# Kernel rows of a long convolution: two channels per matmul, group 2's rows and skip term earlier, one butterfly moved to TensorE

## The chip, the cores and the metric

The kernel runs on one core of one Trainium2 chip. The metric is the device time of one execution in microseconds (us). A second table of times comes from the hardware profiler, which records one execution of the program.

Engines: TensorE (PE; its weight loads are listed as PEld), VectorE (DVE), ScalarE (ACT), GpSimd (POOL) and SyncE (SP, which here only issues transfers). Each engine takes its instructions in the order of its own queue. An instruction that waits holds up all that stand behind it.

## What is computed

One block of a network: two residual halves, each with an adaptive layer norm. The first half is a long convolution along time (a state-space layer, S4D), the second a feed-forward layer. L = 2048 positions, D = 576 channels, N = 128 states, 4608 hidden units, all in float32.

```python
dt = exp(log_dt); A = -exp(log_A_real) + 1j * A_imag; C = (C_real + 1j * C_imag) * dt[:, None]
P = exp((A * dt[:, None])[:, :, None] * arange(L))       # D x N x L
K = 2.0 * einsum("dn,dnl->dl", C, P).real                # one kernel of 2048 taps for each channel
y = irfft(rfft(u_t, 2 * L) * rfft(K, 2 * L))[:, :, :L]   # causal convolution
A_ref = y + u * D_skip                                   # the skip term
...
h = layernorm(x) * (1 + ca) + sa;  x = x + ga * A_ref(h)
h = layernorm(x) * (1 + cb) + sb;  x = x + gb * (relu(h @ w1) @ w2)
```

The skip term is the same as adding D_skip to the tap at lag 0 of each channel's kernel K.

## The kernel before

**The taps of K ("kernel rows").** A power of e at position l = 32 a + j splits into a factor for a and a factor for j. `KGen` builds both on chip: W2 (32 fine steps, two parts r, 48 channels) and W1 (16 coarse steps). The product of W2 and W1 over the 128 states is one small matmul for each channel and part: 32 weight columns, 16 moving columns (`products`, L254, the matmul at L264). The first 512 taps of all channels are made this way in six groups of 96 channels (g = 0 to 5); groups 0 to 2 give the even half p = 0 of the channels, groups 3 to 5 the odd half p = 1. In `products` the four channels of a step go to four strips of 32 output partitions, so four column tiles of TensorE are in use. A float32 matmul shows as two instructions with two weight loads: 2304 are recorded where the code issues 1152.

For a group g, `first` (L273) issues in this order: `values(g)` (sines, cosines and exponentials on ScalarE, products on VectorE and POOL, giving W2, and the powers Z), `double(g)` (W1 from one coarse step by four doublings on VectorE, with the last one's additions on POOL), `multiply(g)` (the matmuls into one PSUM bank, from a pair of banks that `bank` deals out in turn), and `rows(g)` (ScalarE copies the bank into the tile ke). After three groups `store` writes ke to DRAM (kd, two transfers on SP). W2, W1 and Z are also saved to DRAM, because the later taps (512 to 2047) are made from them during the feed-forward part; some of these saves are held back and issued later.

What sets the order: ScalarE's and POOL's instructions of `KGen` keep the order of the program (`act` L55, `pool` L58). From `conv0` on, `kept` (L499) also pins VectorE's, SP's and part of the other engines' work in the order written. The rest is ordered by a scheduler when the program is built.

**The convolution of the first 512 positions** (`conv0`, L1099 and on) uses transforms of length 512 made of matmuls and butterflies. `transform` (L757) makes four products of one half each for real and imaginary part: ZU from the normed input h, ZK from the rows kt, which come back from kd by `load_kt` in another arrangement. `butterfly1` (four additions of 128x576) and `butterfly2` (six) on VectorE make the spectra U0 and K0. Then `product` gives Y, a butterfly gives V, and `inverse` (ps_i) goes back by matmuls. `transform1` (L793) is a transform that has `butterfly1` inside: each result is a sum of two matmuls, with a table that has its sign turned where the butterfly subtracts. It serves the second half's rows (WK). Before each kt is used, `src_K` adds D_skip to its lag-0 row, on VectorE for the first half (L515, the line of the helper `v`) and on POOL for the second (L1138).

In `conv0` the generator `first` is resumed between these steps: doubling of group 4, then group 4's products one piece at a time between the pieces of ZK's transform (`between`), doubling of group 5, group 5's products. VectorE's queue there is: doubling of group 4, the addition to kt, doubling of group 5, butterfly of ZU (W, then U0), butterfly of ZK (W, then K0), Y, V, the butterflies of the second half's input (U1), K1 from WK, and so on.

Then follow the layer norm of these positions and the feed-forward part, four blocks of 512 positions, with the later blocks' convolutions between its matmuls (hps L1334, acc L1359). Names that the prediction uses: W1, W2, Z (`Zp`, `zs`) are factors of K; `cc` holds C; `fcU`, `fcK`, `early` are tables of the transforms; `in_neg` holds tables with turned sign; `wm` are weights of the layer norms' modulation.

## Time and profile before

| | us |
|---|---|
| median of 3 runs | 1343.76 |
| lowest, highest | 1338.28, 1344.12 |
| the profiled execution | 1342.5 |
| its span, first to last instruction | 1340.7 |

Over the whole span TensorE is busy 91%, VectorE 65%, ScalarE 38% and POOL 15%; the mean granted clock of TensorE is 0.949 of full speed.

How to read the lines. A timeline line has the start in us, the time in us that the line covers, the engine, the source line, the operation, the tiles (out<-in), their shapes and how many instructions are merged in it; in square brackets, how long the engine stood idle before it and who released it. SPq is SyncE's queue of transfers, and its time is that of issuing. A line of a table of windows gives a stretch, its length, then the busy time and the number of instructions of PE, PEld, DVE, ACT and POOL, the granted clock, the share of the DMA engines in use and GB/s. A line of a table of groups gives source line, engine, operation, tiles, shapes and count, then busy time and the mean of one in ns, then the idle time before them. A line of transfers gives issues, KB of each and median us from issue to landing.

### The profile page before, as it was taken

How to read it: one execution, taken by the hardware profiler on the slowest of the kernel's cores; microseconds unless marked ns; L12 is line 12 of the kernel's file. 1: busy time of each engine (PE TensorE's matmuls, PEld its weight loads, DVE VectorE, ACT ScalarE, POOL GpSimd, SP SyncE). 2: the span in 40 equal slices, each digit the busy share in tenths (PEclk: the TensorE clock that was granted, in tenths of full speed). 3: DMA queues.
4: the chain of work that ended last, by engine and by line, in shares of the span. 5: the costliest groups of instructions: out<-in, count | busy, mean ns of one | idle time of the engine just before them, and what ended most of it. 6: DMA issues, size and time to landing. Idle time of an engine off the chain costs nothing.

```text
span 1340.7 us, 26038 instructions
## 1 busy us (share of the span) xinstructions
PE 1218.8 (91%) x10608; PEld 972.3 (73%) x10608; DVE 869.8 (65%) x1351; ACT 504.2 (38%) x1014; POOL 195.2 (15%) x271
## 2 busy tenths in 40 slices
PE   5125699899999998999999999999999999999998
PEld 3124567678787786777777786787888888888886
DVE  5998898999887898289447885366988222111111
ACT  7987124222224323522243225343322353232331
POOL 1788131111120000111101100100010000000000
PEclk9555799899999998999999999999999999999999
DMA  6666499888898876698779893758997556666651
GB/s 199 246 248 248 145 362 407 303 281 302 293 357 283 291 253 209 222 384 309 245 255 332 289 372 117 264 182 275 318 348 237 169 178 213 196 199 200 196 168 62
DMA packets 132424, 340.47 MB, mean 254 GB/s; under 512 B 22352, under 2 KB 22672, under 8 KB 132304
## 3 DMA queue, kind: packets, MB, share of 16 engines
q1 hardware_dynamic: 105200, 215.21, 48.7%
q0 software_dynamic: 26816, 123.01, 25.1%
q8 instruction: 83, 1.36, 0.4%
q10 hardware_dynamic: 288, 0.59, 0.1%
q14 instruction: 37, 0.30, 0.1%
HBM read 258.55 MB, written 80.22 MB: 253 GB/s over the span
## 4 chain that ended last, share of the span: by engine, by line
PE 71%; DVE 12%; DMA 8%; issue 6%; POOL 2%; ACT 2%; SPq 0%; DVEq 0%; ACTq 0%; POOLq 0%
PE hps L1334 28%; PE acc L1359 27%; PE kps L445 5%; PE ps_f L764 3%; DVE T L515 3%; DVE Y L515 3%; DMA Ua<-Ud 3%; PE kps L264 2%; PE ps_i L1025 2%; DVE W L515 1%; PE kps L612 1%; DMA Ka<-Rd 1%; DMA Zr<-Zd 1%; DMA wm_gb<-in_w_mod_dram 1%; POOL W L59 1%
## 5 line engine op out<-in xcount | busy, mean ns | idle before, releaser
L1359 PE MATMUL acc<-hh,w 128*128 128x512 f32 x1296 | 422.2, 400 | 2.1 <-DVE w L515 2.0
L1334 PE MATMUL hps<-xh,w 128*128 128x512 f32 x1152 | 395.0, 403 | 0.7 <-ACT xh L1090 0.4
L1359 PEld LDWEIGHTS acc<-hh,w 128*128 128x128 f32 x1296 | 243.4, 189 | 55.3 <-DVE w L515 2.8
L1359 PE MATMUL acc<-hl,w 128*128 128x512 f32 x720 | 281.1, 400 | 0.0
L1340 DVE SCALAR_TENSOR_TENSOR hl<-hps,hh 128x512 fp32r<-128x512 f32 x144 | 98.9, 687 | 278.1 <-ACT hh L1339 277.8
L1334 PEld LDWEIGHTS hps<-xh,w 128*128 128x128 f32 x1152 | 218.1, 190 | 48.6 <-ACT xh L1090 1.8
L1334 PE MATMUL hps<-xl,w 128*128 128x512 f32 x576 | 230.7, 401 | 0.2 <-DVE xl L1095 0.2
L1339 ACT ACTIVATE hh<-hps 128x512 fp32r<-128x512 f32 x144 | 86.2, 598 | 328.4 <-PE hps L1334 323.8
L1312 ACT ACTIVATE w<-r 128x576 fp32r<-128x576 f32 x144 | 98.8, 687 | 237.8 <-issue 183.1
L1359 PEld LDWEIGHTS acc<-hl,w 128*128 128x128 f32 x720 | 135.8, 189 | 28.3
L1334 PEld LDWEIGHTS hps<-xl,w 128*128 128x128 f32 x576 | 109.4, 190 | 25.1 <-DVE xl L1095 1.5
L1305 ACT ACTIVATE w<-r 128x640 fp32r<-128x640 f32 x142 | 103.9, 732 | 16.7 <-DMA r<-in_w_dram 15.9
L264 PE MATMUL kps<-W,W 128*32 128x16 f32 x2304 | 40.1, 217 | 76.0 <-POOL W L59 46.9
L1334 PE MATMUL hps<-xs,w 128*128 128x512 f32 x288 | 97.7, 419 | 2.2 <-DVE hl L1340 2.0
L264 PEld LDWEIGHTS kps<-W,W 128*32 128x32 f32 x2304 | 37.7, 150 | 80.5 <-POOL W L59 48.1
L515 DVE TENSOR_TENSOR Y<-Y,T 128x1152 f32<-128x1152 f32 x64 | 85.0, 1352 | 0.1
L445 PEld LDWEIGHTS kps<-W1r,W2r 128*32 128x32 f32 x3456 | 63.8, 146 | 27.9 <-issue 21.6
L445 PE MATMUL kps<-W1r,W2r 128*32 128x48 f32 (+2 forms) x3456 | 71.3, 237 | 8.4 <-issue 7.3
L765 ACT ACTIVATE Z<-ps_f 128x288 f32<-128x288 f32 x104 | 42.4, 408 | 64.5 <-PE ps_f L764 62.3
L1334 PEld LDWEIGHTS hps<-xs,w 128*128 128x128 f32 x288 | 53.7, 192 | 15.0 <-DVE hl L1340 3.1
L515 DVE TENSOR_TENSOR W<-Z 128x576 f32<-128x576 f32 x52 | 37.0, 754 | 40.6 <-ACT Z L765 40.6
L515 DVE TENSOR_TENSOR w<-r,w 128x512 fp32r<-128x512 f32 (+2 forms) x108 | 58.0, 573 | 3.3 <-ACT w L1312 3.0
(215 smaller groups left out, 1361.9 us busy)
## 6 DMA issues: line engine op xcount, KB each, us to landing
r<-in_w_dram SPq DMA_DIRECT2D x144, 320.0 KB, 4.1
r<-in_w_dram SPq DMA_DIRECT2D x144, 288.0 KB, 3.7
w<-L1d SPq DMA_DIRECT2D x108, 320.0 KB, 3.0
w<-L2d SPq DMA_DIRECT2D x108, 288.0 KB, 3.1
W2r<-W2d POOLq DMA_DIRECT2D x18, 1536.0 KB, 9.2
W2d<-W SPq DMA_DIRECT2D x10, 1536.0 KB, 7.4
W<-W1d POOLq DMA_DIRECT2D x18, 768.0 KB, 9.2
Ua<-Ud POOLq DMA_DIRECT2D x12, 1152.0 KB, 10.4
```

The lines of the kernel that those rows point to most:

```text
L264: self.nc.tensor.matmul(ps[32 * dd : 32 * dd + 32, 12 * u + q, :], W2[:, r, :, ch], W1[:, u, :, r, ch], start=(r == 0), stop=(r == 1),)
L445: nc.tensor.matmul(ps[32 * dd : 32 * dd + 32, q, :], W2[:, r, :, ch], W1[:, :na, r, ch], start=(r == 1), stop=(r == 0),)
L515: return self.kept(self.nc.vector.tensor_tensor(*args, **kw))
L764: kept(nc.tensor.matmul(o, fc[:, n2, c, :], src(n2), start=True, stop=True))
L765: nc.scalar.activation(Z[:, n2, c], ps[:, :PC], AF.Copy)
L1025: self.nc.tensor.matmul(ps[:, :PC], a, b, start=(i == 0), stop=(i == len(todo) - 1))
L1305: nc.scalar.activation(w[:, 0], r, AF.Copy)
L1312: nc.scalar.activation(w[:, 0:D], r2[g], AF.Copy)
L1334: nc.tensor.matmul(ps, a, x, start=(i == 0), stop=(i == 13))
L1339: nc.scalar.activation(hh, ps, AF.Relu)
L1340: nc.vector.scalar_tensor_tensor(hl, ps, 0.0, hh, op0=ALU.max, op1=ALU.subtract)
L1359: nc.tensor.matmul(acc[i], a, x, start=(f == 0 and j in (0, 3, 6, 9, 12)), stop=(f == NF - 1 and j in (2, 5, 8, 11, 13)),)
```

## The change

1. `pairs` takes the place of `products` for groups 3, 4 and 5. One matmul holds two channels: 64 weight columns (fine steps of both), 32 moving columns (coarse steps of both), into 64 output partitions. Of the four blocks of its output, the two in which the weights and the moving columns belong to the same channel are used. A group then fills two PSUM banks, which are evicted one at a time, into a ke with twice the columns, and the store of p = 1 takes the blocks that are used, in four transfers on SP's and ScalarE's queues.
2. The skip term is loaded at the start (three small loads on POOL's queue) and added to ke before it is stored: on VectorE for p = 0, on POOL for p = 1. `src_K` adds nothing any more.
3. `rows(2)`, its store and the loads of `early` move to the middle of `values(4)`; `multiply(3)` moves behind `values(4)`; the rows of p = 0 are loaded (kt0, in the buffer of `cc`) in the middle of `values(5)`, and group 4's saves of W2 and Z are issued behind that load. `rows(4)` moves ahead of `multiply(5)`.
4. The first half's input is transformed by `transform1` instead of `transform` and `butterfly1`. For that a third table with turned sign is made on the host and loaded into the first half of `fcU`; `cb` and `row` of the modulation, and `gcn`, move into free parts of `fcU` and `fcK`.

```diff
@@ -83,9 +83,15 @@
         self.a, self.th = (self.pa.tile([P, D], F32, name=n) for n in ("lar", "th"))
         ai = self.pt.tile([P, D], F32, tag="T1", bufs=2, name="ai")
         dt = self.pt.tile([P, D], F32, tag="T0", bufs=2, name="dt")
-        self.cc = pc.tile([P, 2, D], F32, name="cc")
+        self.cc = pc.tile([P, 2, D], F32, tag="cc", bufs=1, name="cc")
         self.halfpi = pc.tile([P, 1], F32, name="halfpi")
         nc.vector.memset(self.halfpi, math.pi / 2)
+        self.skip = pc.tile([P, 2, 72], F32, name="skip")
+        nc.gpsimd.memset(self.skip, 0.0)
+        dv = I["dsk"].rearrange("(dd p q) -> p dd q", dd=4, p=2)
+        nc.gpsimd.dma_start(out=self.skip[::32, 0], in_=dv[0])
+        for x in range(2):
+            nc.gpsimd.dma_start(out=self.skip[x::64, 1], in_=dv[1, 2 * x : 2 * x + 2])
         nc.sync.dma_start(out=dt, in_=I["ldt"].unsqueeze(0).to_broadcast([P, D]))
         nc.scalar.dma_start(out=ai, in_=I["ai"])
         nc.scalar.dma_start(out=self.a, in_=I["lar"])
@@ -270,6 +276,26 @@
                         )
                     )
 
+    def pairs(self, banks, W1, W2s, between):
+
+        for u in range(2):
+            a = W2s[u].rearrange("p r j (x c) -> p r (j x) c", x=2)
+            b = W1[:, u].rearrange("p a r (x c) -> p r c x a", x=2)
+            for q in range(12):
+                if q % 6 == 3:
+                    for _ in range(2):
+                        next(between, None)
+                for r in range(2):
+                    for half in range(2):
+                        c = 12 * half + q
+                        o = banks[u][64 * half : 64 * half + 64, 32 * q : 32 * q + 32]
+                        self.mm = self.kept(
+                            self.nc.tensor.matmul(
+                                o.rearrange("p (x a) -> p x a", x=2), a[:, r, :, c], b[:, r, c],
+                                start=(r == 0), stop=(r == 1),
+                            )
+                        )
+
     def first(self, setup, mod, norm):
 
         nc, k = self.nc, self.k
@@ -306,15 +332,22 @@
             self.half_values(g, W2, E[2:4], F[0], True)
             then()
             self.half_values(g, W2, E[0:2], F[1], False)
+            if g != 4:
+                saves(g, 0)
+            self.powers(g, E[4], F[2])
+            if g != 4:
+                saves(g, 1)
+
+        def saves(g, i):
             for u in range(2):
-                save(
-                    strips(k.W2d[2 * g + u], 4),
-                    W2[u].rearrange("p r (y b) c -> p (r y) (b c)", y=2), g == NG - 1,
-                )
-            self.powers(g, E[4], F[2])
-            zs = self.Z[g][1]
-            for u in range(2):
-                save(k.Zd[2 * g + u], zs[:, :, :, u * H : u * H + H], g == NG - 1)
+                if i:
+                    zs = self.Z[g][1]
+                    save(k.Zd[2 * g + u], zs[:, :, :, u * H : u * H + H], g == NG - 1)
+                else:
+                    save(
+                        strips(k.W2d[2 * g + u], 4),
+                        W2s[g][u].rearrange("p r (y b) c -> p (r y) (b c)", y=2), g == NG - 1,
+                    )
 
         def double(g, steps=range(4)):
             self.doubling(g, steps)
@@ -328,17 +361,58 @@
 
         def multiply(g, between=iter(())):
             self.kept = k.kept if g == NG - 2 else lambda x: x
+            if g > 2:
+                kps[g] = [self.bank() for _ in range(2)]
+                self.pairs(kps[g], self.W1[g], W2s[g], between)
+                return
             kps[g] = self.bank()[:, :384].rearrange("p (q a) -> p q a", a=16)
             for u in range(2):
                 self.products(kps[g], self.W1[g], W2s[g][u], u, between)
 
         def rows(g):
             if g % 3 == 0:
-                ke[0] = self.pc.tile([P, 16, 72], F32, tag="ke", bufs=1, name=f"ke_{g}")
-            qs = slice(24 * (g % 3), 24 * (g % 3) + 24)
-            self.act(ke[0][:, :, qs], kps.pop(g).rearrange("p q a -> p a q"), AF.Copy)
-            if g % 3 == 2:
-                self.store(0, g // 3, ke[0].rearrange("p a q -> p (a q)"), nc.sync)
+                ke[0] = self.pc.tile([P, 2, 16, 72], F32, tag="ke", bufs=1, name=f"ke_{g}")
+            t = ke[0]
+            q0 = 24 * (g % 3)
+            if g < 3:
+                self.act(t[:, 0, :, q0 : q0 + 24], kps.pop(g).rearrange("p q a -> p a q"), AF.Copy)
+            else:
+                for u, ps in enumerate(kps.pop(g)):
+                    self.act(
+                        t[:, :, :, q0 + 12 * u : q0 + 12 * u + 12],
+                        ps[:, :384].rearrange("p (q x a) -> p x a q", x=2, a=16), AF.Copy,
+                    )
+            if g == 2:
+                nc.vector.tensor_tensor(t[:, 0, 0], t[:, 0, 0], self.skip[:, 0], op=ALU.add)
+                self.store(0, 0, t[:, 0].rearrange("p a q -> p (a q)"), nc.sync)
+            elif g == 5:
+                nc.gpsimd.tensor_tensor(
+                    t[:, :, 0], t[:, :, 0],
+                    self.skip[:, 1].unsqueeze(1).broadcast_to([P, 2, 72]), op=ALU.add,
+                )
+                f = t.rearrange("p x a q -> p x (a q)")
+                for y in range(2):
+                    for x, eng in enumerate((nc.sync, nc.scalar)):
+                        k.kept(eng.dma_start(
+                            out=k.kd[0][1][64 * y + 32 * x : 64 * y + 32 * x + 32],
+                            in_=f[2 * y + x :: 4, x],
+                        ))
+
+        def ahead():
+            rows(2)
+            t = k.early = self.pc.tile([P, 2, 4, 2, P], F32, tag="W1", bufs=4, name="early")
+            for i, n in enumerate(("fcu", "fck")):
+                nc.sync.dma_start(out=t[:, i], in_=k.I[n])
+
+        def head(g):
+            if g == 0:
+                rows(0)
+            double(g + 2, range(2))
+            if g == 2:
+                k.kt0 = self.pc.tile([P, 16, 72], F32, tag="cc", bufs=1, name="kt0")
+                nc.sync.dma_start(out=k.kt0, in_=k.kd_rows(0, 0))
+                for i in range(2):
+                    saves(4, i)
 
         load, stats, scale, center, affine = norm
         next(mod)
@@ -352,15 +426,15 @@
         values(1, lambda: None)
         for g in (0, 2):
             raw(g // 2 + 1)
-            for i in (g, g + 1):
-                double(i, range(2, 4) if i == 2 else range(4))
-                multiply(i)
-            values(g + 2, lambda: None)
-            if g == 2:
-                t = k.early = self.pc.tile([P, 2, 4, 2, P], F32, tag="W1", bufs=4, name="early")
-                for i, n in enumerate(("fcu", "fck")):
-                    nc.sync.dma_start(out=t[:, i], in_=k.I[n])
-            values(g + 3, lambda: (rows(g), double(g + 2, range(2))))
+            double(g, range(2, 4) if g else range(4))
+            multiply(g)
+            double(g + 1)
+            if g == 0:
+                multiply(1)
+            values(g + 2, ahead if g else lambda: None)
+            if g:
+                multiply(3)
+            values(g + 3, lambda: head(g))
             rows(g + 1)
             if g == 0:
                 for i in (2, 3):
@@ -372,8 +446,8 @@
         yield
         double(5)
         yield
+        rows(4)
         multiply(5)
-        rows(4)
         rows(5)
 
     def store(self, s, p, ke, eng):
...
@@ -1111,10 +1186,8 @@
         cpsa = self.cps, self.nps = self.pool(c, "cpsa", space=PSUM), 2
         cpsa = cpsa[0]
         self.half_tag = "kt"
-        self.dsk = self.fcU[0:1].rearrange("p a b c -> p (a b c)")[:, :D]
-        nc.gpsimd.dma_start(out=self.dsk, in_=I["dsk"].unsqueeze(0))
-        fcKn = self.fcK.rearrange("p a b c -> p (a b) c")[:, 0:4]
-        gcn = cva.tile([P, 4, P], F32, name="gcn")
+        fcUn, fcKn = (t.rearrange("p a b c -> p (a b) c")[:, 0:4] for t in (self.fcU, self.fcK))
+        gcn = self.fcK.rearrange("p a b c -> p (a b) c")[:, 4:]
         self.pinned = True
 
         def behind(d, op):
@@ -1128,18 +1201,16 @@
             return self.kept(nc.sync.dma_start(out=t, in_=a))
 
         early = self.early
-        kt = [self.load_kt(0, 0)]
+        load(fcUn, I["neg"][2])
+        kt = [self.kt0]
         hv = self.h.rearrange("m n (dd p q) -> m n dd p q", dd=4, p=2)
 
         def src_K(p):
             ktv = kt[p].rearrange("p (t dd g) q -> p t dd g q", t=2, g=2)
-            dv = self.dsk.rearrange("o (dd p q) -> o dd p q", dd=4, p=2)[:, :, p]
-            add = nc.gpsimd.tensor_tensor if p else self.v
-            add(ktv[0:1, 0, :, 0], ktv[0:1, 0, :, 0], dv, op=ALU.add)
             return lambda n2: ktv[:, n2 // 2, :, n2 % 2]
 
-        ZU, ZK = S(0, "ZU"), S(1, "ZK")
-        run(self.transform(lambda n2: hv[:, n2, :, 0], early[:, 0], ZU))
+        WU, ZK = S(2, "WU"), S(1, "ZK")
+        run(self.transform1(lambda n2: hv[:, n2, :, 0], early[:, 0], fcUn, WU))
         next(first)
         ZKs = self.transform(src_K(0), early[:, 1], ZK, self.kept)
         first.send(ZKs)
@@ -1149,10 +1220,8 @@
             behind(d, kg.mm)
         next(first)
         kg.factors.close()
-        W = S(2, "W")
-        run(self.butterfly1(ZU, W))
         U0 = S(0, "U0")
-        run(self.butterfly2(W, U0, -1))
+        run(self.butterfly2(WU, U0, -1))
         self.save(self.Ud[0][0], U0)
         W = S(3, "W")
         run(self.butterfly1(ZK, W))
...
-         np.stack([r["gc"][:, n, c] for n, c in ((1, 0), (2, 0), (2, 1), (3, 1))], axis=1)]
+         np.stack([r["gc"][:, n, c] for n, c in ((1, 0), (2, 0), (2, 1), (3, 1))], axis=1),
+         r["fcu"][:, 2:].reshape(P, 4, P)]

```

More of the change, by code (lines that the diff above doesn't have):

```diff
@@ L617, in mod_late @@
         cv = self.cv
-        cb = cv.tile([P, 5, 32], F32, name="cb")
+        spare = self.fcU[:, 2:].rearrange("p a b c -> p (a b c)")
+        cb = spare[:, : 5 * 32].rearrange("p (k r) -> p k r", k=5)
+        row = spare[:, 256:]
         self.kept(nc.vector.tensor_copy(cb, self.ct.unsqueeze(2).broadcast_to([P, 5, 32])))
@@ L645, in mod_late @@
                 yield
-            row = cv.tile([P, 2 * P], F32, tag="row", bufs=1, name=f"row_{nm}")
             act(row[:, 0:P], ps[:, 0:P], AF.Copy)
@@ L1262, in conv0, with kd_rows @@
         self.half_tag = "T"
+    def kd_rows(self, s, p):
+        kd = self.kd[s][p]
+        return bass.AP(tensor=kd.tensor, offset=kd.offset, ap=[[72, P], [9216, 16], [1, 72]])
     def load_kt(self, s, p):
         kt = self.cv.tile([P, 16, 72], F32, tag="kt", bufs=1 if s else 2, name="kt")
[L1266 to L1270 removed]
+        d = (self.nc.gpsimd if s else self.nc.sync).dma_start(out=kt, in_=self.kd_rows(s, p))
         if s == 0:
```

5 lines of the change are left out of this document (removed).

## The prediction

> **What bounds the kernel now.** I read the table of windows first, to see where the change can act. Columns: stretch, its length, busy time of PE, weight loads, DVE, ACT and POOL, granted clock, DMA share, GB/s.
>
> ```profile
> span 1340.7 us, 26038 instructions
> ...
> 139.00:172.00 33.00, 25.73 (x760) 20.37 (x761) 32.59 (x55) 7.58 (x18) 4.13 (x5) 0.84 0.45 148
> 172.00:182.00 10.00, 10.00 (x43) 7.85 (x42) 8.09 (x15) 2.88 (x7) 6.37 (x7) 1.00 1.05 390
> 182.00:209.40 27.40, 23.98 (x217) 17.08 (x216) 25.98 (x53) 11.44 (x32) 7.74 (x11) 0.90 1.02 399
> 209.40:1340.70 1131.30, 1107.31 (x7934) 886.78 (x7933) 693.36 (x935) 371.34 (x662) 89.66 (x128) 0.99 0.75 255
> ```
>
> From 209.4 us on TensorE is busy for 1107.31 of 1131.30 us and the change touches nothing there. Everything edited lies ahead of it, and there VectorE is the full engine: 32.59 of 33.00 us between 139 and 172, 25.98 of 27.40 after 182. So a microsecond taken out of VectorE's chain before 209.4 moves the whole feed-forward part forward by one, provided nothing else (TensorE's chain, a transfer) arrives later than VectorE then does. I therefore walked the timeline along VectorE from 108 us, and beside it the two things it waits for, TensorE and the kernel rows that go out to DRAM (kd) and come back (kt).
>
> ```profile
> 138.66 0.45 DVE L515 TENSOR_TENSOR kt<-kt,fcU 1x288 f32<-1x288 f32 x1 [5.16 <-DMA kt<-kd]
> 139.03 0.34 DVE L515 TENSOR_TENSOR t<-W,Zp 128x192 f32<-128x192 f32 x1
> ...
> 149.79 2.76 DVE L515 TENSOR_TENSOR W<-ZU 128x576 f32<-128x576 f32 x4
> 152.58 2.90 DVE L515 TENSOR_TENSOR U<-W 128x576 f32<-128x576 f32 x6
> 155.40 2.76 DVE L515 TENSOR_TENSOR W<-ZK 128x576 f32<-128x576 f32 x4
> 168.99 2.77 DVE L515 TENSOR_TENSOR V<-Y 128x576 f32<-128x576 f32 x4
> 181.59 2.90 DVE L515 TENSOR_TENSOR K<-WK 128x576 f32<-128x576 f32 x6 [1.80 <-ACT WK L804]
> ...
> 209.46 1.20 PE L1334 MATMUL hps<-xs,w 128*128 128x512 f32 x2
> ```
>
> VectorE stands still for 5.16 us until the first rows are back, adds the skip term, and only then doubles group 5, which needs no rows at all: it is merely queued behind the addition. Then it runs without a break to V at 168.99 and K at 181.59.
>
> **Part 1, the rows of group 2.** Today they are evicted, stored and loaded like this:
>
> ```profile
> 118.15 0.47 ACT L56 ACTIVATE ke<-kps 128x384 f32<-128x384 f32 x1
> 117.72 2.36 SPq L298 DMA_DIRECT2D W2d<-W  x2
> 120.86 2.56 SPq L298 DMA_DIRECT2D Zd<-zs  x2
> 125.53 1.97 SPq L382 DMA_DIRECT2D kd<-ke  x2
> 133.20 0.36 SPq L1267 DMA_DIRECT2D kt<-kd  x1
> ```
>
> The store stands on SP's queue behind group 4's four saves, so rows evicted at 118.15 leave at 125.53 and are loaded at 133.20. The change evicts between the two halves of group 4's values, stores ahead of the `early` loads, and puts the four saves behind the new load of kt. The addition then sits ahead of the store, 128x72 on VectorE; the smallest additions here are a 0.34 us row of 128x192, so at most that.
>
> ```profile
> 108.25 0.83 ACT L56 ACTIVATE c<-k 128x768 f32<-128x768 f32 x1
> 109.63 2.15 PE L264 MATMUL kps<-W,W 128*32 128x16 f32 x127 [1.83 <-issue]
> 110.69 0.50 ACT L56 ACTIVATE s<-k 128x384 f32<-128x384 f32 x1 [1.62 <-DVE W L174]
> 111.77 0.55 DVE L173 TENSOR_TENSOR W<-s,E 128x384 f32<-128x384 f32 x1
> 113.85 2.15 PE L264 MATMUL kps<-W,W 128*32 128x16 f32 x128 [2.07 <-issue]
> 118.68 2.13 PE L264 MATMUL kps<-W,W 128*32 128x16 f32 x128 [2.68 <-issue]
> 119.50 0.56 DVE L173 TENSOR_TENSOR W<-s,E 128x384 f32<-128x384 f32 x1 [1.93 <-PE kps L264]
> 120.44 0.34 DVE L180 TENSOR_TENSOR tc<-cc,s 128x192 f32<-128x192 f32 x1
> ```
>
> ScalarE keeps program order, so this is an added wait: group 2's products end some way into the batch that starts at 109.63, at about 111.3, the eviction takes 0.47, and the absolute value that runs at 108.25 starts only near 111.9. Queued behind it are the sines; the one at 110.69 moves to about 112.7, and its reader on VectorE from 111.77 to some 113, plus the small addition. Cost: 1.2 us. Against it stands the wait of 1.93 us at 119.50: a W2 buffer of group 5 is free only when the first half of group 3's products is done, and that half shrinks (part 2). The two together lie between 1.9 gained and 1.2 lost; POOL paces the next steps too, so I take 0.5 gained.
>
> The load of kt takes the buffer of cc, which VectorE reads last at 120.44. So it is issued near 120.8, not 133.20, and should land near 126 by the 5.4 us from 133.20 to 138.6. VectorE has no business with it any more: it goes from doubling group 4 (done at 138.66 - 5.16 = 133.5) straight to group 5. Gain: 139.03 - 133.5 = 5.5 us. The constant term itself costs three small loads and a clearing on POOL in the first microseconds, where nothing waits for POOL; I count nothing, at worst a microsecond if POOL were late.
>
> **Part 2, two channels in one matmul.**
>
> ```profile
> L264 PE MATMUL kps<-W,W 128*32 128x16 f32 x2304 | 40.1, 217 | 76.0 <-POOL W L59 46.9
> ...
> 241.84 2.30 PE kps L445 x90
> ```
>
> 2304 matmuls in six groups are 384 a group; the change makes 192 of groups 3, 4 and 5, each with 64 weight columns and 32 moving ones, half of whose output is thrown away. A 32-column, 16-wide one costs 2.15 / 128 = 16.8 ns at its best, and every 128 of them are followed by about two to three microseconds without instructions ("issue"). The new form isn't in the trace. Bounds: no less than 16.8 ns (same rate of issue); no more than 67 ns: four column tiles share 16.8 ns, so one tile turns a matmul over in 67 ns; if twice the columns on both sides cost 134 ns and only two tiles remain, that is 67 apiece. The nearest row is the 32-column, 48-wide products later on, 2.30 / 90 = 25.6 ns, and I take that: 4.9 us a group, from 3.2 to 12.9. Eviction is 2 x 0.48 instead of one, on a ScalarE with 7.58 us to do in 33.
>
> This alone is not on VectorE's path; it decides when ZK and the second rows are there (part 4).
>
> **Part 3, U0's first butterfly.** Four additions, 149.79 to 152.58, leave VectorE: 2.8 us. TensorE pays: eight accumulations of two instead of eight single products. Prices:
>
> ```profile
> 127.16 5.83 PE L764 MATMUL ps_f<-h,early 128*128 128x288 f32 x16
> 174.15 0.65 PE L801 MATMUL ps_f<-kt,early 128*128 128x288 f32 x2
> 182.11 0.41 ACT L804 ACTIVATE WK<-ps_f 128x288 f32<-128x288 f32 x1 [0.56 <-PE ps_f L803]
> 143.00 1.24 PE L764 MATMUL ps_f<-kt,early 128*128 128x288 f32 x4
> 149.71 2.81 PE L264 MATMUL kps<-W,W 128*32 128x16 f32 x170
> ...
> W2d<-W SPq DMA_DIRECT2D x10, 1536.0 KB, 7.4
> ...
> fcK<-in_neg_dram SPq DMA_DIRECT2D x1, 256.0 KB, 3.3
> ```
>
> The like transform of WK takes 182.1 - 174.15 = 8 us, or 1 us a sum, against 5.83 now. It also needs a negated table, a new load on SP behind kt and the four saves: 120.8 + 2.36 + 2.56 = 125.7. Its landing takes 3.3 us (a table of the same size, quiet queue) to 7.4 (the big save): 129 to 133. I take 130, nearer the small one. The second sum already needs it, so U ends at 130 + 7 = 137, not 133. VectorE wants the result at 149.8 - 6.0 = 143.8, so this is covered by 6 us.
>
> **Part 4, what is late next.** ZK and group 4's products follow U on TensorE: 4 x 1.24 = 5.0 us of transform and 4.9 of products, the last transform after seven eighths of them: 137 + 5.0 + 4.3 + 0.4 (its eviction) = 146.7. VectorE wants ZK at 155.4 - 0.5 - 5.5 - 2.8 = 146.6. Just met; at 12.9 us a group it is 7 us late. Then group 5's products, after their doubling (143) and the banks' eviction: 147.4 to about 152.5. From there to kt of the second rows:
>
> ```profile
> 163.38 0.49 ACT L56 ACTIVATE ke<-kps 128x384 f32<-128x384 f32 x1 [12.17 <-PE kps L264]
> 163.90 1.38 SPq L382 DMA_DIRECT2D kd<-ke  x2
> 168.50 0.38 SPq L1267 DMA_DIRECT2D kt<-kd  x1
> 173.22 2.08 POOL L1138 TENSOR_TENSOR kt<-kt,fcU 1x288 f32<-1x288 f32 x1 [11.07 <-DMA kt<-kd]
> ...
> 169.80 3.54 PE L1025 MATMUL ps_i<-V,gc 128*128 128x288 f32 x12 [0.84 <-DVE V L515]
> ```
>
> Now 9.8 us (163.38 to 173.2); then POOL's addition stands ahead of the store instead of behind the load, and there are four stores on two queues. I add 1 us (0 to 2.1, the POOL row): 163.3. TensorE takes WK after the first ps_i, which starts 0.8 us behind V and lets WK go 5.2 us after V. V comes at 168.99 - 8.8 = 160.2, so WK may start at 165.4: the rows have 2 us to spare, and the 1.80 us wait before K stays as it is.
>
> **The sum.** 0.5 + 5.5 + 2.8 = 8.8 us: K at 172.8, the first feed-forward matmul near 200.7. The profiled execution took 1342.5 us (span 1340.7), 1.3 under the median of 1343.76. So 1342.5 - 8.8 = 1333.7, and on the scale of the medians **1335.0 us**.
>
> **The rivals.** *TensorE late.* The table lands at 133 behind the saves: U ends at 140, ZK at 149.7, VectorE stops for 3.1 us: 5.7 gained, 1338.1. For it: TensorE takes its instructions in order, and ZK has 0.1 us to spare. Against: TensorE is idle for microseconds now, and the saves may be ordered otherwise.
>
> *Transfers hold it.* DMA share is 1.05 and 1.02 from 172 to 209.4; if those bytes can't start sooner, most of the gain ends in waits for weights before 209: about 3 left, 1341. Against: they are set off by the same steps that move forward.
>
> *The wide matmul is dear (slower).* At 67 ns, ZK comes at 153.7, group 4 ends at 155, group 5 at 168; the second rows are there at 168 + 10.8 = 178.8, WK 8 us later, K at 187 instead of 181.59: 5.4 us lost, 1349.2. The point where it turns: K unmoved needs group 5 done at 162.6, which is 384 matmuls in 20.6 us, 53 ns each. Only two column tiles instead of four speaks for it; that the 16.8 ns is the same in batches at half clock (113.85) and later (149.71: 2.81 / 170), so the array isn't what limits, speaks against. The Trainium skill ("TensorEngine Tiling (Array Packing)", Available Configurations) lists four tiles for 128x32 and two for 128x64, which is this rival's case; by it alone the time would be the 1349.2. No row here shows the 64-column mode.
>
> *The change does less:* U0's edit alone counts if kt still lands late; but VectorE no longer waits for kt, so even then ZK, not the wait, decides, and that is the first rival.
>
> **How the numbers follow.** A measurement here tells about 0.5%, 6.7 us: faster is under 1337.0, slower over 1350.5. Forecast with its 7 to 10 us: 0.52. TensorE late: 0.25, a fifth of it still under 1337. Transfers: 0.10. Wide matmul: 0.13, of which about half goes past 1350.5 if half-clock batches add to it. Faster 0.57, same 0.36, slower 0.07. Low end: the 8.8 with the whole 1.9 of part 1 and a WK wait shortened by 1.8 is 12 gained: 1331.8, so 1331. High end: no gain, 1344. That leaves out the dear matmul's 0.13 and a little below.
>
> **What would show it.** Right: no wait of VectorE on kt and no row kt<-kt; group 5's first doubling near 133; no W<-ZU; V near 160, K near 173, first hps near 201. In TensorE, rows of 128*64 with 128x32, 576 of them, near 25 ns apart. Wrong: a wait before W<-ZK of over 3 us (first rival); WK waiting on kt past 165 and a group over 10 us (third); K early but hps not (second).

## The result, and the profile after

| | before | after |
|---|---|---|
| median, us | 1342.38 (6 runs) | 1354.28 (6 runs) |
| lowest, highest | 1338.28, 1344.12 | 1349.12, 1355.60 |
| the profiled execution, its span | 1342.5, 1340.7 | 1355.6, 1353.8 |
| group 5's products end | 163.35 | 176.6 |
| K of the second rows starts | 181.59 | 197.43 |
| first hps | 209.46 | 224.84 |

The six runs of before are the three above and three more. The ratio is 1.0088, 95% interval 1.0067 to 1.0109: 12 us slower where 8.8 us faster was forecast. The table of windows of the kernel after, first over the stretches where VectorE used to be the full engine:

```profile
139.00:172.00 33.00, 32.99 (x325) 26.78 (x324) 20.44 (x31) 6.59 (x16) 4.17 (x5) 0.60 0.31 110
172.00:182.00 10.00, 10.00 (x92) 8.62 (x91) 6.45 (x9) 2.95 (x7) 0.48 (x1) 0.65 0.08 30
182.00:209.40 27.40, 22.56 (x167) 16.25 (x165) 17.83 (x26) 6.58 (x19) 8.51 (x12) 0.94 0.97 355
```

VectorE is busy for 20.44 us of 33 where it was for 32.59, and TensorE for 32.99 where it was for 25.73. The full engine has changed. The granted clock fell from 0.84 to 0.60, and DMA has 0.08 to do between 172 and 182 where it had 1.05: everything behind waits for one chain. The timeline of that chain:

```profile
112.88 0.49 ACT L56 ACTIVATE ke<-kps 128x384 f32<-128x384 f32 x1 [3.23 <-PE kps L270]
121.30 0.38 SPq L413 DMA_DIRECT2D kt<-kd  x1
127.39 3.79 SPq L1201 DMA_DIRECT2D fcU<-in_neg_dram  x1
133.82 0.45 PE L293 MATMUL kps<-W,W 128*64 128x32 f32 x4 [1.52 <-POOL W L59]
134.33 0.35 DVE L589 TENSOR_TENSOR t<-W,Zp 128x192 f32<-128x192 f32 x1
134.80 1.48 PE L293 MATMUL kps<-W,W 128*64 128x32 f32 x20 [0.52 <-POOL W L59]
136.21 2.29 PE L878 MATMUL ps_f<-h,fcU 128*128 128x288 f32 x4
...
145.09 3.24 PE L293 MATMUL kps<-W,W 128*64 128x32 f32 x48
148.26 2.29 PE L839 MATMUL ps_f<-kt,early 128*128 128x288 f32 x4
150.48 3.25 PE L293 MATMUL kps<-W,W 128*64 128x32 f32 x48
...
161.84 1.43 DVE L589 TENSOR_TENSOR W<-ZK 128x576 f32<-128x576 f32 x2 [9.38 <-ACT ZK L840]
164.21 12.38 PE L293 MATMUL kps<-W,W 128*64 128x32 f32 x192
174.10 2.76 DVE L589 TENSOR_TENSOR V<-Y 128x576 f32<-128x576 f32 x4
177.71 1.12 SPq L396 DMA_DIRECT2D kd<-ke  x2
179.49 1.86 ACT L840 ACTIVATE Z<-ps_f 128x288 f32<-128x288 f32 x4 [0.24 <-PE ps_f L839]
181.01 1.14 ACTq L396 DMA_DIRECT2D kd<-ke  x2
183.85 0.38 SPq L1339 DMA_DIRECT2D kt<-kd  x1
197.43 2.90 DVE L589 TENSOR_TENSOR K<-WK 128x576 f32<-128x576 f32 x6 [4.38 <-ACT WK L879]
```

The first rows do what was foreseen: evicted at 112.88, their kt is loaded from 121.30, and doubling 5 starts at 134.33 with no wait for it (predicted 133). Then four things go wrong. The table for U0 is only issued at 127.39, and TensorE takes up the sum that needs it at 136.21, behind the first 24 of group 4's matmuls. Each 48 of group 4's wide matmuls take 3.25 us, or 68 ns one (matmuls are counted as recorded, two for each in the code). Group 5 takes 12.38 us for 192, 64.5 ns one. Of the four stores of the second rows, SP's two leave at 177.71, but ScalarE's two stand behind its evictions of Z until 181.01, and the load of kt comes at 183.85. What VectorE now waits for between 139 and 200, in the table of waits (total, times, longest):

```profile
DVE W L589 <- ACT ZK L840: 12.4, 2, 9.4
DVE K L589 <- ACT WK L879: 4.4, 1, 4.4
DVE x L589 <- DMA x<-in_x_dram: 4.3, 1, 4.3
DVE W L589 <- ACT Z L840: 4.1, 2, 2.8
```

All four stand for something that TensorE, or a transfer behind its results on SP's queue, delivers late.

### The profile page after: what moved, and what is told of

Same layout as the page of the kernel before. It is cut to its first block, busy times and chain, and to the rows that moved or that the text cites. A ratio compares the mean times of both kernels' runs of the same rounds, so it can differ in the third digit from the quotient of the medians.

```text
span 1353.8 us, 24933 instructions
## 1 busy us (share of the span) xinstructions
PE 1245.0 (92%) x10048; PEld 994.9 (73%) x10048; DVE 867.6 (64%) x1347; ACT 504.8 (37%) x1017; POOL 195.0 (14%) x274
## 4 chain that ended last, share of the span: by engine, by line
PE 72%; DVE 11%; DMA 6%; issue 5%; ACT 3%; POOL 2%; SPq 0%; ACTq 0%; DVEq 0%; POOLq 0%
PE hps L1403 28%; PE acc L1428 28%; PE kps L519 5%; PE ps_f L839 5%; DMA r<-in_w_dram 2%; DVE T L589 2%; DVE Y L589 2%; PE kps L293 2%; DMA Ua<-Ud 2%; POOL W L59 2%; PE ps_i L1100 1%; PE kps L686 1%; DMA Ka<-Rd 1%; DVE k L140 1%; DVE T L255 1%
## 5 line engine op out<-in xcount | busy, mean ns | idle before, releaser
L1403 PEld LDWEIGHTS hps<-xl,w 128*128 128x128 f32 x576 | 109.0, 189 | 25.6 <-DVE xl L1170 2.3
L589 DVE TENSOR_TENSOR Y<-Y,T 128x1152 f32<-128x1152 f32 x64 | 85.0, 1352 | 0.1
L519 PEld LDWEIGHTS kps<-W1r,W2r 128*32 128x32 f32 x3456 | 63.7, 146 | 26.7 <-issue 20.3
L270 PE MATMUL kps<-W,W 128*32 128x16 f32 x1152 | 20.0, 216 | 59.9 <-POOL W L59 46.2
L270 PEld LDWEIGHTS kps<-W,W 128*32 128x32 f32 x1152 | 18.8, 150 | 61.4 <-POOL W L59 47.0
```

The costliest lines, as they stand in the source:

```text
L270: self.nc.tensor.matmul(ps[32 * dd : 32 * dd + 32, 12 * u + q, :], W2[:, r, :, ch], W1[:, u, :, r, ch], start=(r == 0), stop=(r == 1),)
L519: nc.tensor.matmul(ps[32 * dd : 32 * dd + 32, q, :], W2[:, r, :, ch], W1[:, :na, r, ch], start=(r == 1), stop=(r == 0),)
L589: return self.kept(self.nc.vector.tensor_tensor(*args, **kw))
L1403: nc.tensor.matmul(ps, a, x, start=(i == 0), stop=(i == 13))
```

## The experiments

Theory A: a matmul of 64 weight columns costs about 65 ns because its time goes with its weight columns and only two can run side by side. Theory B: the late table is what costs. A rival to both: the early rows or the four stores cost. Each ratio is to runs of the kernel before on the same chip. A time is a median of several runs, a trace is of one: the traced execution took 1342.62 us in e2_pairs, 1336.60 in e3_rows and 1351.87 in e4_u0, some way off their medians.

**e1_singles.** The change, but with one channel in a matmul for all six groups, as before. The eviction to one bank and the store on SP's queue alone come back with it; that part of the edit isn't printed.

```diff
...
-            if g > 2:
-                kps[g] = [self.bank() for _ in range(2)]
-                self.pairs(kps[g], self.W1[g], W2s[g], between)
-                return
...
```

> The change with one channel per matmul in groups 3 to 5 again (384 matmuls a group into one bank, eviction and store as before); early rows, skip term and U0's transform stay as changed. Theory 'wide matmul' (the 64.5 ns of a two-channel matmul are the whole loss): the rest of the change keeps its 8.8 us, about 1334 us, K from WK near 173. Rival 'late table' (the table with turned sign lands at 136 behind group 4's saves, and TensorE's queue waits for it): U's transform still ends near 143, ZK near 154, group 5 near 167, K near 185, so 3 to 5 us slower than before, about 1346.

Measured: 1340.70 us, ratio 1.0003 (0.9987 to 1.0020). The whole loss goes with the wide matmuls and what comes with them, but no gain is left either. Its timeline:

```profile
127.52 3.78 SPq L1180 DMA_DIRECT2D fcU<-in_neg_dram  x1
...
135.51 2.29 PE L857 MATMUL ps_f<-h,fcU 128*128 128x288 f32 x4
143.74 1.68 PE L269 MATMUL kps<-W,W 128*32 128x16 f32 x96
```

96 narrow matmuls take 1.68 us where 48 wide ones took 3.25. The table comes as late as in the change, and U's transform is as late here too. Group 5 is done at 168.4, 8.2 us sooner than in the change. That isn't won in group 5: behind the last of ZK's pieces the 432 narrow matmuls take 16.2 us here, with four stops of 1.3 to 4.0 us ("issue"), and the 216 wide ones 15.3 us there, with a sum of 1.3 us between. It is won in group 4's pieces, three times 1.6 us, in ZK's pieces (5.3 us for 8.3), three of which run at half clock in the change, and 1.4 us in U.

The edit takes away something else that neither theory names, the two stores on ScalarE's queue. In the change the load of kt comes 6.1 us behind SP's stores (177.71 to 183.85; SP's queue waits 4.8 us of it for the stores), here 3.3 us (169.35 to 172.61). From the end of group 5 to K it is 20.8 us in the change, 17.8 here and 18.2 before: 3.0 of the 11.2 us by which K comes sooner here. One queue for the stores, with the wide matmuls kept, was not tried.

**e2_pairs.** The kernel before, with the wide matmuls of groups 3 to 5 alone. Their two banks, the four stores, `rows(4)` ahead of `multiply(5)` and the moves of `cb`, `row` and `gcn` come with them; that part of the edit isn't printed.

```diff
...
+            if g > 2:
+                kps[g] = [self.bank() for _ in range(2)]
+                self.pairs(kps[g], self.W1[g], W2s[g], between)
+                return
...
```

> The kernel before with the two-channel matmuls of groups 3 to 5 alone (two banks, eviction, four stores on two queues as in the change; rows of group 2, skip term and U0 as before). Wide matmul: group 4 and 5 take 12.4 us each, ZK near 157, group 5 ends near 171, K near 191: about 10 us slower, 1352. Late table: there is no such table here, so within 3 us of before.

Measured: 1347.15 us, ratio 1.0047 (1.0024 to 1.0071). Its timeline, where ZK's transform and groups 4 and 5 share TensorE:

```profile
145.31 3.25 PE L287 MATMUL kps<-W,W 128*64 128x32 f32 x48
148.49 2.29 PE L805 MATMUL ps_f<-kt,early 128*128 128x288 f32 x4
...
156.10 13.89 PE L287 MATMUL kps<-W,W 128*64 128x32 f32 x216
```

13.89 / 216 = 64.3 ns again. Three of the four pieces of ZK's transform take 2.29 us here, at a granted clock of 0.50, and one 1.37. Before, one takes 2.26 us and three 1.24. That is 2.3 us more. All four stores leave at 170.56 here and the load at 174.44, so ScalarE's queue costs nothing in this run.

**e5_forms.** The change, with a form of its own for each group: group 3 keeps 64 weight columns but moves 16 columns (384 matmuls); group 4 has 32 weight columns and moves 32 (384 matmuls over four strips); group 5 is the change's form with both parts r of one half behind each other.

```diff
...
+                    if g == 3:
+                        parts = [(o[:, x], A, B[:, x]) for x in xs]
+                    elif g == 4:
+                        parts = [(o[32 * s : 32 * s + 32], A[:, 32 * s : 32 * s + 32], B) for s in range(2)]
+                    else:
+                        parts = [(o, A, B)]
...
```

> The change with another form of the two-channel product in each of three groups, so that the ns per matmul can be read from the trace; the work is cut differently, the result is the same. Group 3: 64 weight columns, 16 moving, 384 matmuls. Group 4: 32 weight columns, 32 moving, 384. Group 5: 64 and 32 as in the change, 192, but both parts r of one strip one behind the other, as in the kernel before. If it is the number of column tiles: group 3 near 33 ns (two tiles instead of four), group 4 near 20, group 5 near 64. If it is the alternation of strips: group 5 falls to about 20. If it is the moving columns: group 4 near 33 and group 3 near 17.

Measured (one execution, 1348.14 us): the table of groups by form, and a timeline row of group 4.

```profile
L308 PE MATMUL kps<-W,W 128*64 128x16 f32 x384 | 26.4, 288 | 0.0
L308 PE MATMUL kps<-W,W 128*64 128x32 f32 x192 | 12.4, 299 | 0.0
```

```profile
153.34 1.82 PE L308 MATMUL kps<-W,W 128*32 128x32 f32 x96
```

Moving 16 columns instead of 32 saves nothing: 26.4 / 384 = 69 ns, where the readings named 33 or 17. Halving the weight columns cuts 64.5 ns to 1.82 / 96 = 19 ns, though 32 columns still move. So the price is the weight columns', and it falls by more than half, since four strips share it instead of two. The windows of these stretches:

```profile
110.60:136.90 26.30, 26.30 (x386) 26.23 (x384) 20.04 (x50) 13.06 (x25) 20.91 (x31) 0.50 0.76 267
...
160.90:173.10 12.20, 12.20 (x192) 12.16 (x192) 12.06 (x15) 0.79 (x2) 0.76 (x1) 1.00 0.53 185
```

Group 3 ran at a granted clock of 0.50 and group 5 at 1.00, at nearly the same price, and group 5 of the change took the same 12.38 us at 0.50. The price doesn't follow the clock. Weight loads (second busy column) are recorded for 12.16 of 12.20 us; whether the load or the matmul behind it sets the pace was not separated.

**e6_forms2.** The same for three other forms: group 3 with 128 weight columns, group 4 with 32 columns strip by strip (48 matmuls on one strip, then the next), group 5 with 64 columns half by half.

```diff
...
+            if g == 3:
+                todo = [(q, 0, 128, r) for q in range(12) for r in range(2)]
+            elif g == 4:
+                todo = [(q, 32 * s, 32, r) for s in range(4) for q in range(12) for r in range(2)]
+            else:
+                todo = [(q, 64 * s, 64, r) for s in range(2) for q in range(12) for r in range(2)]
...
```

> Forms again, in the changed kernel. Group 3: 128 weight columns (four channels) and 32 moving, 96 matmuls; two of the four blocks that a channel needs are left out, so its taps are not the reference's. Group 4: 32 columns and 32 moving, all of one strip before the next. Group 5: 64 and 32, all of one half before the other. If small matmuls are fast because four strips run side by side, group 4 slows from 18.9 to 50 ns or more and group 5 stays near 64. If only 32-column weights are loaded beside the running matmul, group 4 stays near 19, group 5 near 64, and group 3 costs more than 64.

Measured (one execution, 1378.24 us), in the timeline:

```profile
112.82 25.93 PE L306 MATMUL kps<-W,W 128*128 128x32 f32 x96
...
160.97 6.16 PE L306 MATMUL kps<-W,W 128*32 128x32 f32 x96
...
179.37 20.81 PE L306 MATMUL kps<-W,W 128*64 128x32 f32 x174
```

With no other strip at work beside it a matmul takes 64 ns with 32 weight columns, 120 with 64, 270 with 128 (the last measured at a granted clock of 0.50 only): 2 ns a column. Four strips side by side bring 64 to 16.8 or 19, two bring 120 to 64.5. Group 5 at 120 was not expected by either reading. Together this bears out theory A, and gives the simple account of a group: 384 x 32 and 192 x 64 are the same number of weight columns, spread over four strips or over two.

**e7_table.** The change, with the third table loaded between the two `early` loads (group 2's middle), not behind kt and the saves.

```diff
...
+            nc.sync.dma_start(out=t[:, 0], in_=k.I["fcu"])
+            nc.sync.dma_start(out=k.neg, in_=k.I["neg"][2])
+            nc.sync.dma_start(out=t[:, 1], in_=k.I["fck"])
...
-        load(fcUn, I["neg"][2])
```

> The change, with the table with turned sign loaded between the two loads of early (at about 116 us) instead of behind group 4's saves (127.4). Wide matmul: U's transform ends near 135 instead of 143.5, everything after it 8 us sooner, but the groups still take 12.4 us: about 1348, still 5 us slower than before. Late table: the loss is gone, 1334 to 1340.

Measured: 1347.78 us, ratio 1.0041 (1.0019 to 1.0062), 6 us better than the change. U's last sum is evicted at 134.1 instead of 143.9, group 5 ends at 167.8, and

```profile
187.23 2.90 DVE L592 TENSOR_TENSOR K<-WK 128x576 f32<-128x576 f32 x6 [2.06 <-ACT WK L882]
```

K starts at 187.2, 10.2 us sooner. Theory B has its share: about half of the loss. With narrow matmuls the same move is worth some 4 us (1.0003 in e1_singles, 0.9973 in e8_singles_table below). What holds U's transform in the change is more than the landing itself. With the late table, group 4's first 24 matmuls stand ahead of the sum in TensorE's queue, and they wait for POOL's W until 133.82 (timeline above); with the early table U is through before them. In e6_forms2 the sum starts at 147.13, behind 48 such matmuls, though the table, issued at 133.19, takes 8.0 us and is there by 141.2.

**e8_singles_table.** Both at once: one channel in a matmul, and the early table. The edit is that of e1_singles and of e7_table.

> The change with one channel per matmul again and the table with turned sign loaded between the two loads of early. Both causes named so far are out: if they are the whole loss, U's transform ends near 134, ZK near 145, group 5 near 158, K near 177 and the first hps near 205, 5 us sooner than before; the time then 1336 to 1339. Rival (what is gained ahead of the feed-forward part doesn't reach the end: in the run with single channels alone hps came 5 us later and the time stayed): hps sooner, time within 2 us of before.

Measured: 1338.20 us, ratio 0.9973 (0.9956 to 0.9991): a little faster than the kernel before, clear of the noise. V starts at 162.23, 6.8 us ahead of before, but K only at 184.75, behind before's 181.59. Its timeline shows why:

```profile
163.80 0.78 POOL L812 DMA_DIRECT2D Rd<-K  x1
163.88 1.12 SPq L438 DMA_DIRECT2D kd<-ke  x2
171.23 0.38 SPq L1320 DMA_DIRECT2D kt<-kd  x1
```

The addition of the skip term stands on POOL's queue ahead of the save of K0's spectrum (Rd, 1152 KB). K0 was ready at 154.3, the save waited for group 5's eviction, and it went out beside the stores of the second rows, which then took 7.3 us to the load behind them (4.6 before).

**e3_rows** and **e4_u0.** The early rows with the skip term alone (single channels, U0's butterfly on VectorE); and U0's butterfly in TensorE alone, with the table among the `early` loads.

```diff
-                self.pairs(kps[g], self.W1[g], W2s[g], between)
...
-        run(self.transform1(lambda n2: hv[:, n2, :, 0], early[:, 0], fcUn, WU))
+        run(self.transform(lambda n2: hv[:, n2, :, 0], early[:, 0], ZU))
...
+        run(self.butterfly1(ZU, W))
```

> The early rows and the skip term alone (one channel per matmul, U by four products and a butterfly on VectorE as before, no new table). VectorE's 5.5 us wait on kt goes, ZK starts behind U at 133 and ends near 144, group 5 near 157, K near 176: hps 5 us sooner, time 1336 to 1339. Rival: TensorE's chain through group 5 and the second rows gives part of it back (K no sooner than 179), time within 2 us of before.

```diff
-        run(self.transform(lambda n2: hv[:, n2, :, 0], early[:, 0], ZU))
+        run(self.transform1(lambda n2: hv[:, n2, :, 0], early[:, 0], self.neg, WU))
...
-        run(self.butterfly1(ZU, W))
```

> U0's first butterfly in TensorE alone, with its table loaded early; rows, skip term and products as before. VectorE loses 2.8 us of work before ZK's butterfly (152.6 instead of 155.4), ZK is there at 150.2: K near 179.5, about 2 us gained, 1339 to 1341. Rival 'late table', read as 'the longer transform itself is dear': ZK waits for TensorE, no gain or a loss of 2.

Measured: 1344.58 us, ratio 1.0014 (0.9993 to 1.0036) for the rows, 1341.07 us, ratio 0.9994 (0.9975 to 1.0013) for U0. Neither is worth anything that shows by itself. In e4_u0 the table stands on SP's queue ahead of the store of the first rows, which leaves at 129.76 instead of 125.53; VectorE's wait for kt stays (4.99 us). In e3_rows POOL's queue did the same as in e8, for two saves:

```profile
159.46 0.32 POOL L377 TENSOR_TENSOR ke<-ke,skip 128x72 f32<-128x72 f32 x1 [15.37 <-ACT ke L56]
159.73 0.81 POOL L809 DMA_DIRECT2D Ud<-U  x1
...
166.14 2.76 DVE L568 TENSOR_TENSOR V<-Y 128x576 f32<-128x576 f32 x4 [2.48 <-DMA Ud<-U]
```

V takes U0's buffer and so waits for its save.

**e10_rd_first.** e8_singles_table, with the addition bound to stand behind the save of K0.

```diff
+                k.tc.add_manual_dep(add.ins, k.saved.ins.name, ..., reason="behind")
```

> The version with single channels and the early table, with one order changed: POOL saves the spectrum K0 (Rd, 1152 KB) as soon as it is there, ahead of the addition of the skip term to the second rows, and no longer right behind it. In the version before this one Rd went out at 163.80 and the stores of the second rows at 163.88; they landed at 171.1. Theory 1 (the two share the transfer engines, and that is what makes the stores late): Rd is issued near 154.5 and is through by about 161.5, the stores land within 4.6 us of 163.9, so by 168.5; kt is loaded from 168.6 and lands near 173, WK is done near 182.5 and K starts near 182, 2.7 us earlier than 184.75. Time 1335.5 us, ratio to before 0.9953. Theory 2 (the stores are slow by themselves, or wait for other transfers): they land near 171 again, K starts near 184.8, time 1338.2, ratio 0.9973.

Measured: 1336.09 us, ratio 0.9954 (0.9935 to 0.9973), the time that theory 1 of that run gave, and the lowest ratio of all versions. The timeline:

```profile
156.82 0.76 POOL L819 DMA_DIRECT2D Rd<-K  x1 [4.80 <-DVE K L578]
161.39 0.53 POOL L377 TENSOR_TENSOR ke<-ke,skip 128x72 f32<-128x72 f32 x1 [3.81 <-ACT ke L56]
...
161.94 1.12 SPq L445 DMA_DIRECT2D kd<-ke  x2
165.18 0.38 SPq L1329 DMA_DIRECT2D kt<-kd  x1
...
178.00 2.90 DVE L578 TENSOR_TENSOR K<-WK 128x576 f32<-128x576 f32 x6 [2.58 <-ACT WK L870]
```

From store to load it is 3.2 us now instead of 7.3, and K starts at 178.0. That is 6.8 us sooner than in e8_singles_table and 4 sooner than theory 1 said, while the time falls by 2.5 us, by the ratios.

**e9_no_u0** and **e11_no_u0_saves.** The change without its fourth part (wide matmuls and early rows remain); then the same with the addition bound behind both saves, as in e10.

```diff
-        run(self.transform1(lambda n2: hv[:, n2, :, 0], early[:, 0], fcUn, WU))
+        run(self.transform(lambda n2: hv[:, n2, :, 0], early[:, 0], ZU))
...
+        run(self.butterfly1(ZU, W))
```

> The change without its fourth part: U0's first butterfly stays on VectorE, no third table; the two-channel matmuls, the early rows of group 2 and the skip term stay. Theory 1 (the late table is all that the butterfly's move costs, the wide matmuls are the rest): the time lies with the version whose table is early, 1347 us, ratio 1.003 to 1.006, group 5's products end between 167 and 170, first hps near 216. Theory 2 (the late table only uncovers a cost that the four stores on two queues and the two-bank evictions have anyway): the time stays near that of the change, 1352 or more, ratio 1.008 and over.

```diff
+                for d in k.saved:
+                    k.tc.add_manual_dep(add.ins, d.ins.name, ..., reason="behind")
```

> The change without U0's butterfly in TensorE, as in the run before, and in addition POOL issues the saves of U0 and K0 (Ud, Rd) ahead of the addition of the skip term to the second rows; there both were queued behind it until 173.8, and V waited 10.4 us for Ud's landing, since it takes U0's buffer. Theory 1 (that queue order is the price seen in that run): no wait of V on Ud, V starts near 170.3, the stores of the second rows land by 178, kt near 182.5, K near 191 and not 194.9: time 1353.5 us, ratio 1.0085. Theory 2 (the early rows and the wide matmuls without U0's move cost no more than with it and an early table): 1347 us, ratio 1.004, K near 187.

Measured: 1357.71 us, ratio 1.0108 (1.0071 to 1.0145), and 1352.74 us, 1.0089 (1.0057 to 1.0121), four runs each. By its time the first lies where theory 2 had it (1352 or more), and 1347 is missed; but its trace shows a cause that neither theory names. The timeline of e9_no_u0:

```profile
173.42 0.48 POOL L389 TENSOR_TENSOR ke<-ke,skip 128x144 f32<-128x144 f32 x1 [24.25 <-ACT ke L56]
173.85 0.81 POOL L830 DMA_DIRECT2D Ud<-U  x1
...
180.64 2.76 DVE L589 TENSOR_TENSOR V<-Y 128x576 f32<-128x576 f32 x4 [10.38 <-DMA Ud<-U]
```

The saves again, and with them put ahead V starts at 167.44 and K at 191.48 (194.93 in e9_no_u0): theory 1 of the second run, which named 1353.5. The intervals of the two runs overlap. With POOL's queue in order, theory 2 of the first run has its part after all: in e11_no_u0_saves SP's stores leave at 171.06, ScalarE's at 175.12, behind evictions of Z as in the change, and the load comes at 178.00. In the change itself both saves happened to go out first (148.28 and 166.50, the addition at 177.20), so POOL's queue is no part of its loss. In time, 1.0089 without U0's move stands beside 1.0088 with it and 1.0041 with an early table: so late, the table eats what the move seems to be worth. That this worth is VectorE's butterfly isn't shown: in e11_no_u0_saves K waits 3.89 us for WK, so TensorE's chain and the stores decide there.

**e12_rows_saves.** e3_rows with the addition bound behind both saves, by the same lines as in e11_no_u0_saves.

> Early rows of group 2 and the skip term alone, single channels, U0's butterfly on VectorE, with Ud and Rd issued by POOL ahead of the addition to the second rows. Without that order both went out behind it, at 159.73 and 160.54, beside the stores of the second rows (159.81), V waited 2.48 us for Ud, and the stores landed at 166.3. Theory 1 (the early rows do save VectorE's wait, and the moved addition gave it back by holding two saves on POOL's queue): V starts near 163.7, the stores land by 164.4, kt by 169.3, WK is done near 177.5 and K starts near 178, 3.6 us ahead of before: 1338 us, ratio 0.9975. Theory 2 (the rows' move is worth nothing at the end): 1341 to 1344.6, ratio 1.000 to 1.0014.

Measured: 1339.84 us, ratio 0.9992 (0.9972 to 1.0012). The trace has theory 1's landmarks (V at 165.59 without a wait, K at 178.19 for an expected 178, first hps at 205.67, 3.8 us ahead of before), and the time has not followed: the interval holds both theories. The windows of the 90 us from the first hps on, in this kernel:

```profile
205.67:295.67 90.00, 80.83 (x1023) 63.66 (x1024) 80.65 (x85) 25.36 (x44) 12.67 (x19) 0.94 0.87 319
```

TensorE stands still for 9.17 us of these 90. In the kernel before it was 6.5 us of the 90 us from its first hps on, in the change, which gets there 15.4 us later, 4.5. So in these executions part of what is won ahead of the first hps is given back in waits right behind it; which waits these are is left open.

## Why the prediction was wrong

**The step that failed is part 2's price.** It took 25.6 ns from the 32-column, 48-wide products, as the "nearest row", and so 4.9 us a group; measured are 64.5 ns and 12.4 us. The row was near in the wrong dimension: it has the old weight columns and more moving columns. e5_forms shows that 16 or 32 moving columns cost nearly the same and that the weight columns set the price; at 48 moving columns the old form takes 24 ns in the kernel before. (The row is the part of a batch of 96 that lies on the critical chain: 2.30 / 96 is 24 ns, not 25.6.) The upper bound of 67 ns was right, and for the right reason (twice the columns, half the strips), but for the word "both": only the columns on the weight side count. The argument that set it aside was "the 16.8 ns is the same in batches at half clock and later, so the array isn't what limits". The observation holds: the windows of the change show 48 wide matmuls at 1.00 and at 0.50 in the same time.

```profile
145.10:148.20 3.10, 3.10 (x49) 3.10 (x48) 2.88 (x7) 0.41 (x1) 0.60 (x1) 1.00 0.20 56
...
150.50:153.60 3.10, 3.10 (x49) 3.09 (x48) 1.43 (x2) 0.41 (x1) 0.00 (x0) 0.50 0.71 271
...
148.30:176.40 28.10, 28.10 (x328) 24.03 (x326) 15.85 (x20) 4.13 (x10) 1.56 (x2) 0.50 0.34 123
```

But a price that ignores the clock may still grow with the shape. The conclusion did not follow, and with it the third rival got 0.13 where it should have led. That rival said K at 187 and 1349.2 us; e2_pairs and e7_table have K at 187.2 and 1347.15 and 1347.78. So close a match is partly luck: in e7_table U is done 3 us sooner than the rival had it, and two of ZK's pieces run at half clock, 2.1 us that it didn't have. The rule of the Trainium skill that the prediction weighed ("TensorEngine Tiling (Array Packing)", Available Configurations: four tiles of 128x32, two of 128x64) is borne out by these runs.

**Part 3's landing was missed by 5.5 us.** The table was to be issued at 125.7 and to land at 130, at worst at 133. It was issued at 127.39 and took 8.1 us, by the row of transfers:

```profile
fcU<-in_neg_dram SPq DMA_DIRECT2D x1, 256.0 KB, 8.1
```

That is 135.5, past the worst of the range: of the two rows it was priced by (3.3 and 7.4 us), the longer was the nearer. The table stands behind four saves, and the DMA share is 1.03 from 127.4 to 131.5 and 0.64 from there to 135.5. "Covered by 6 us" counted only VectorE's need of U; TensorE, which takes its instructions in order, had group 4's first 24 matmuls ahead of the sum and came to ZK only when U was through at 143.7, not 137. e7_table gives the price: 1.0088 to 1.0041, some 6 us.

**Part 4** had the right chain (U, ZK and group 4, group 5, second rows, WK) with these sizes in it. Group 5's end was put at 152.5 and came at 176.6. The 24 us are 6.7 of U; 7.2 of group 4's 168 matmuls behind U (11.5 us for 4.3); 3.3 of ZK's four pieces, 8.3 us for 5.0, three of them at half clock; 1.3 of a sum of the second half's input that TensorE took in between; 7.5 of group 5. That makes 26, as recorded times overlap a little and the forecast had some slack ahead of group 5. From there to K the forecast had 20.3 us and 20.8 were measured; the four stores, put at 1 us (0 to 2.1), took 1.8 from the eviction to kt (11.6 us for 9.8), with ScalarE's two behind its evictions of Z. The half clock is in no sum; only the chance of the third rival names it. The Trainium skill ("TensorE: Matmul & The Clock Gate", Part 1) has the clock throttled by default and released by some microseconds of sustained activity. This case doesn't bear that out as it stands: in the change TensorE is recorded busy for 28.10 of 28.10 us at 0.50 (last row of the windows above), and e5_forms ran the same form at 1.00. What sets the clock here stays open.

**Part 1 was right** in its mechanism: no wait for kt, doubling 5 at 134.33. The note that nothing waits for POOL held for the first microseconds; that an addition waiting on POOL holds up the saves of U0 and K0 was not looked at. It did not matter in the change. In e8_singles_table, e3_rows and e9_no_u0 the ratios put it at 2.5 to 3 us each; in each of the three pairs of runs the intervals overlap, and only the queue and the waits are plain in the traces. e7_table has it too (Rd at 168.88, the stores at 168.95).

**"A microsecond ahead of 209.4 is one at the end"** held roughly for delays: 15.4 us later at the first hps, 13.1 in the span, 11.9 in the medians. For gains it is doubtful, by e12_rows_saves. Versions with U0's butterfly in TensorE end some microseconds sooner than their first hps tells (e8_singles_table: hps 3.5 us later than before, time 3.6 us lower; e1_singles and e4_u0: hps 5.0 and 4.5 us later, time the same); single executions of one kernel differ by up to 14 us, and this stays open.

With the price of part 2 gone, the table early and POOL's saves ahead of the addition, the rest of the idea was worth 6.2 us (e10_rd_first), against the 8.8 forecast with cheap wide matmuls.

## What to carry to other kernels

Halving the count of small matmuls gained nothing here, where each had twice the weight columns: count weight columns times matmuls, divided by the strips that run side by side. When an operation's shape is not in the trace, ask which dimension the nearest row shares with it, and let a bound that follows from a stated mechanism stand as the forecast until a row speaks against it. A load or an operation put on a queue is priced by what stands ahead of it there, and then by who is queued behind: here a table behind four saves, an addition ahead of two and two stores behind a row of evictions cost as much as the edits gained.

## What the runs showed of the hardware that was not expected

- A small float32 matmul, as recorded, costs about 2 ns for each weight column when no other strip works beside it (64, 120 and 270 ns for 32, 64 and 128, at 32 moving columns). With strips in turn it costs nearly the same for 16 and 32 moving columns (69 and 64.5 ns; 16.8 and 19), and the same at a granted clock of 0.50 and 1.00 (64.5).
- Strips overlap when they take turns within four instructions (64.5 ns with two halves, in either order of r and half), and not when 48 in a row go to one (120 ns).
- Narrow matmuls stop for 0.7 to 5 us between runs of 128 ("issue" in the timelines); 216 wide ones ran without such a stop (e2_pairs). In the kernel before, the 432 narrow matmuls at the end of this chain lasted from 149.71 to 163.35, 13.6 us for 7.5 us of matmuls; the 216 wide ones that do the same took 13.9. So against before the wide form loses nothing there. It loses in group 4's pieces between ZK's, in which the narrow form shows no stop (3.25 us for 1.67, three times), and in the clock of ZK's pieces.
- With one or two 1152 KB saves beside them, it is 6.4 to 7.7 us from the stores of the second rows to the load behind them (e7_table, e3_rows, e8_singles_table, e9_no_u0); 3.2 us in e10_rd_first and e12_rows_saves, where the saves went out sooner.
